# Chaining the shared products of a fast strided convolution and its gradient, and two passes of GELU instead of one for the second batch

## The chip, the cores and the metric

One core of one Trainium2 chip. The metric is the device time of one execution in microseconds (us), the median of the runs shown; lower is better. TensorE (PE) multiplies matrices into PSUM, VectorE (DVE) and ScalarE (ACT) do elementwise work, GpSimd (POOL) clears small ranges and issues some DMAs, and SyncE's queue (SP) issues nearly all DMAs.

## The reference

The forward part is a 1-D convolution with stride 2 and 31 taps over 256 channels, a normalisation of every channel over the sequence, and a tanh-approximated GELU. The kernel returns that output and the four gradients for a given `grad_out`.

```
B, T, D, K = 2, 16000, 256, 31            # L = 7985 outputs per batch
h = einsum('blc,cd->bld', x[:, 0:2*L:2, :], w[0])
for i in range(1, K):
    h = h + einsum('blc,cd->bld', x[:, i:i+2*L:2, :], w[i])
mu  = sum_l h / L
var = sum_l (h - mu)**2 / L
h   = (h - mu) / sqrt(var + 1e-5)
out_0 = gelu(h * gn_gamma + gn_beta)      # approximate=True
# out_1..out_4: gradients of x, w, gn_gamma, gn_beta for grad_out
```

Everything is bf16 in memory; the matmuls accumulate in fp32.

## The kernel before, in words

**Stages.** F is the convolution h (batch 0 is F0, batch 1 is F1), G the gradient of x (G0 and G1), W the gradient of w. Each batch is cut into four chunks, 0 to 3, of 2048 output positions. h and dy (the gradient at the normalised value) go through DRAM tensors `h_d` and `dy_d`.

**A fast convolution.** The tap number is split into bits, i = 8q + 4·r2 + 2·r1 + parity, and on r1, on r2 and on the lowest bit of q a two-by-two product is formed with three products instead of four, from sums and differences of inputs and of weights. The first split gives three *branches* B, A, C (`br`), worked in that order; the second gives three *leaves* B, A, C of each branch (`lf`). Inside a leaf the last split has a *shared product*, which uses a difference table of the weights (`WD`, in G and its counterpart `W2D…`) and counts for the even and the odd outputs alike, and two further products (`f_three_ac`, `g_three_ac`) with input combinations built by `third`. A leaf without that last split is done in full (`f_leaf`, `g_leaf`). One pass over a (batch, chunk, branch) is called a *unit* here; in G a chunk has two halves (`pr` = 0, 1), hence 48 units.

**PSUM.** A unit has two accumulators of two banks, `px` and `pt`; two pairs alternate. Leaf B of a branch is part of both results, so px is first filled with leaf B, then px goes on with leaf A and pt, seeded from px by `f_seed`, with leaf C.

**Units with all three leaves split (`outer`, set `FO`).** 14 of the 24 units of F: all of batch 0 except its very first, and chunk 3 of batch 1. Here `f_three_b` (L524) makes B's shared product and ScalarE spreads it over px with three copies (L540). `f_outer` (L556) makes A's and C's shared products side by side in pt, and ScalarE writes each to SBUF in both signs (`TS`, four copies of 512, L574). For branches A and C, DVE then adds the kept result of branch B (`RB`, fp32) to both (L641, 2048 elements, fp32), and two more DVE operations seed pt and px (L584, L588). `f_evac` moves a finished leaf: branch B into `RB` (L599), A and C into the bf16 tile `hs` with sums (L619) and, after the second leaf, sums of squares (L632).

**G.** Batch 1 has all leaves split (`GOC`, `g_outer`); batch 0 has only leaf B split, and the others go through `g_leaf`. The tables for the split leaves, `W2DC` and `W2DO`, are built by `w2_outer` (L1194, L1197) in the last chunk of batch 0. They lie in the memory (from `GREG` on) in which `gelu_batch` works for batch 1 and, above it, in that of a ring of tiles (`DNO`) from which `dl_turn` stores transposed leaves for W.

**GELU.** `gelu_unit` (L854) handles 1024 positions: it reads h, forms y = scale·h + bias and its square on ScalarE (L864, L866), a cubic on DVE (L869, one `scalar_tensor_tensor`), two sigmoids on ScalarE (L871, L873), then products on DVE (L875, L879): out_0's value y and dy. DVE's L892 and ScalarE's L890 make the sums for the parameter gradients. Batch 0's eight such passes run in F1, batch 1's eight in G0. For batch 1, y goes to DRAM (`y_d`), and `out0_late` (L912) reads it back with a DMA transpose in W and stores out_0. `e_comp` (L967) turns dy and h into the input of G: two scalings, an add on DVE (L985), and four copies by ScalarE into the tile `et` (L994).

**Order.** `Plan.add` collects 3252 operations with their dependences, and `emit` issues them in the order of `SEQUENCE`, a list of all their numbers. That list fixes the order in every queue; each engine and the SP queue then work strictly in that order.

Of the kernel before, what the change touches and what calls it, by code (L numbers as in the profile page):

```python
# [17 lines left out]
GELU_A = 0.044715  # L18
# [213 lines left out]
def conv_stem_kernel(  # L232
# [38 lines left out]
    gamma, beta = gbf[:, 0, :], gbf[:, 1, :]  # L271
    dgb_acc = cpool.tile([P, 2, 2], FP32, name="dgb_acc")
    eps_t = cpool.tile([P, 1], FP32, name="eps_t")
    stats = cpool.tile([P, NB, 8, 2], FP32, name="stats")
    small = cpool.tile([P, NB, 16, 2], FP32, name="small")
    hsum = [cpool.tile([P, 2, 17], FP32, name=f"hsum{b}") for b in range(NB)]
    hsq = [cpool.tile([P, 2, 8], FP32, name=f"hsq{b}") for b in range(NB)]
# [1363 lines left out]
```

## Time and profile before

| | |
|---|---|
| median of 3 runs | 1148.08 us (1147.48 to 1148.45) |
| profiled execution | 1147.09 us, of which its span (first to last instruction) 1145.0 us |
| TensorE clock granted, mean | 0.999 |
| PE busy | 1121.4 us, 98% of the span |
| DVE busy | 943.7 us, 82% |
| ACT busy | 561.7 us, 49% |
| POOL busy | 129.2 us, 11% |
| DMA | 243.56 MB, 213 GB/s on average |

The page of the profile has one row per group of instructions: line, engine, operation, output from input, and count, then busy time, mean ns of one, and idle time of the engine ahead of them with what ended it. Matmuls are pipelined, so the mean ns of one matmul is its latency and not its share of time; the share follows from how many stand in a stretch without a pause. The chain of waits lists, from the last instruction backwards, what released each step. A view by windows gives busy time, granted clock and DMA share in stretches of the span.

### The profile page before, as it was taken

Reading aid. Unit: us, or ns where it says so; the run is one execution under the profiler, and the core shown is the slowest. Engines: PE = TensorE matmul, PEld = TensorE weight load, DVE = VectorE, ACT = ScalarE, POOL = GpSimd, SP = SyncE. Lnnn points to the kernel's source line nnn. Section 1 sums busy time; section 2 is a strip of 40 time slices with the busy share of each in tenths; the row PEclk is TensorE's granted clock in tenths of the full one; section 3 lists DMA queues with packets and bytes.
Section 4 is the critical chain, followed back from the end, with each engine's and each line's share of the span. In section 5 each row is a group of like instructions: output and inputs, shape, how many; then the busy total and the mean of one; then the engine's idle time right before and its main releaser. Section 6 shows DMA issues by size and latency. Waiting matters only on the chain.

```text
span 1145.0 us, 18889 instructions
## 1 busy us (share of the span) xinstructions
PE 1121.4 (98%) x7645; PEld 753.0 (66%) x7700; DVE 943.7 (82%) x880; ACT 561.7 (49%) x873; POOL 129.2 (11%) x221
## 2 busy tenths in 40 slices
PE   5999999999999999999999999999999999999998
PEld 3888899877777874444444444444488766666785
DVE  7997877798999997999887654645599899789995
ACT  1235454777787488888663576754412212112200
POOL 0000000000000012133324325222200000000000
PEclk9999999999999999999999999999999999999999
DMA  9638867958897689999979877577899946989665
GB/s 231 114 80 167 165 161 180 190 123 203 175 207 181 221 333 248 274 268 268 254 185 238 214 204 202 154 191 193 221 302 234 288 149 209 311 260 348 195 218 150
DMA packets 345806, 243.56 MB, mean 213 GB/s; under 512 B 233377, under 2 KB 316967, under 8 KB 341543
## 3 DMA queue, kind: packets, MB, share of 16 engines
q1 hardware_dynamic: 338615, 223.47, 73.9%
q0 software_dynamic: 7104, 18.89, 5.9%
q8 instruction: 60, 0.98, 0.4%
q14 instruction: 27, 0.22, 0.1%
HBM read 106.24 MB, written 80.25 MB: 163 GB/s over the span
## 4 chain that ended last, share of the span: by engine, by line
PE 89%; DVE 7%; ACT 1%; issue 1%; DMA 1%; SPq 0%; DVEq 0%; ACTq 0%
PE ps L504 34%; PE ps L1099 33%; PE ps L1311 22%; DVE arena L1279 1%; DVE arena L1397 1%; DVE ps L1421 1%; DVE arena L1381 1%; DMA out_dram<-arena 1%; DVE arena L1045 1%; DMA arena<-in_x_dram 1%; DVE arena L446 0%; DVE arena L1482 0%; DVE arena L462 0%; ACT arena L994 0%; DVE arena L879 0%
## 5 line engine op out<-in xcount | busy, mean ns | idle before, releaser
L504 PE MATMUL ps<-arena 128*128 128x256 bf16 (+4 forms) x3460 | 406.0, 281 | 12.1 <-DVE arena L446 6.6
L1099 PE MATMUL ps<-arena 128*128 128x512 bf16 x1880 | 408.2, 377 | 3.0 <-DVE arena L1180 0.5
L504 PEld LDWEIGHTS <-arena 128*128 128x128 bf16 x3460 | 338.2, 98 | 79.8 <-DVE arena L446 7.0
L1099 PEld LDWEIGHTS <-arena 128*128 128x128 bf16 x1920 | 188.0, 98 | 222.5 <-issue 2.3
L1311 PE MATMUL ps<-arena 128*128 128x256 bf16 (+1 forms) x2305 | 307.8, 296 | 3.7 <-DVE arena L1477 2.6
L1311 PEld LDWEIGHTS <-arena 128*128 128x128 bf16 x2320 | 226.8, 98 | 84.8 <-issue 3.0
L599 ACT ACTIVATE arena<-ps 128x1024 f32<-128x1024 f32 (+1 forms) x111 | 112.6, 1023 | 234.4 <-PE ps L1311 82.8
L462 DVE TENSOR_TENSOR arena<-arena 128x2064 bf16<-128x2064 bf16 (+8 forms) x126 | 155.7, 1266 | 17.1 <-PE ps L504 16.0
L311 POOL DMA_DIRECT2D dld<-arena x144 | 104.3, 726 | 239.0 <-DMA arena<-arena 194.6
L879 DVE TENSOR_TENSOR arena<-arena 128x2048 bf16<-128x2048 bf16 (+1 forms) x80 | 95.3, 1197 | 8.6 <-ACT arena L871 4.5
L1279 DVE TENSOR_TENSOR arena<-arena 128x4096 bf16<-128x4096 bf16 x38 | 86.4, 2289 | 12.4 <-DMA arena<-in_x_dram 7.8
L1045 DVE TENSOR_TENSOR arena<-arena 128x1032 bf16<-128x1032 bf16 (+1 forms) x108 | 82.2, 791 | 9.7 <-PE ps L1099 9.3
L1162 DVE TENSOR_TENSOR ps<-ps,arena 128x1024 f32<-128x1024 f32 x24 | 29.5, 1231 | 59.0 <-PE ps L1099 36.3
L619 ACT ACTIVATE arena<-ps 128x512 bf16<-128x512 f32 (+1 forms) x64 | 37.1, 582 | 51.9 <-PE ps L504 48.4
L320 POOL MEMSET arena<- 128x128 bf16 (+11 forms) x40 | 8.9, 247 | 446.3 <-DVE arena L879 176.3
L1128 ACT COPY ps<-ps 128x512 f32<-128x512 f32 x72 | 41.5, 577 | 28.4 <-PE ps L1099 25.5
L1413 ACT COPY ps<-ps 128x256 f32<-128x256 f32 x54 | 19.3, 359 | 70.6 <-PE ps L1311 69.5
L574 ACT ACTIVATE arena<-ps 128x512 f32<-128x512 f32 x56 | 30.6, 601 | 44.2 <-PE ps L504 30.5
L869 DVE SCALAR_TENSOR_TENSOR arena<-arena 128x2048 bf16<-128x2048 bf16 (+1 forms) x16 | 35.8, 2240 | 16.7 <-ACT arena L864 10.7
L540 ACT ACTIVATE ps<-ps 128x256 f32<-128x256 f32 x75 | 27.8, 371 | 38.9 <-PE ps L504 38.0
L1180 DVE TENSOR_TENSOR arena<-ps,arena 128x1024 bf16<-128x1024 f32 x32 | 38.9, 1220 | 8.5 <-PE ps L1099 6.4
L1397 DVE TENSOR_TENSOR arena<-arena 128x2048 bf16<-128x2048 bf16 x36 | 43.4, 1222 | 0.1
(84 smaller groups left out, 772.6 us busy)
## 6 DMA issues: line engine op xcount, KB each, us to landing
arena<-in_x_dram SPq DMA_DIRECT2D x40, 1024.0 KB
dld<-arena POOLq DMA_DIRECT2D x144, 128.0 KB, 4.0
arena<-hd SPq DMA_DIRECT2D x32, 512.0 KB
out_dram<-arena SPq DMA_DIRECT2D x14, 1024.0 KB
arena<-dld SPq DMA_DIRECT2D x18, 640.0 KB
arena<-dld SPq DMA_DIRECT2D x18, 576.0 KB
vl<-arena SPq DMA_DIRECT2D x36, 256.0 KB
arena<-vl SPq DMA_DIRECT2D x9, 1024.0 KB
```

What stands on the lines that cost most here:

```text
L311: lambda: e.dma_start(out=out, in_=in_), dma=np_ * ns / 16e3 * 1.03, ns=ns, tp=SH[pk], slack=slack)
L462: lambda: nc.vector.tensor_tensor(out=o, in0=a, in1=b, op=ALU.add))
L504: yield nc.tensor.matmul(ps[:, dh, cs], lhsT=wt, rhs=mv, start=s0, stop=False, skip_group_check=True)
L599: lambda: nc.scalar.activation(out=out, in_=ps, func=ACT.Copy, scale=scale))
L879: add("DVE", dve(nf), [o], [a, b_], lambda: V.tensor_tensor(out=o, in0=a, in1=b_, op=op))
L1045: lambda: nc.vector.tensor_tensor(out=o, in0=a, in1=b, op=ALU.subtract))
L1099: yield nc.tensor.matmul(ps[:, e, 0:wide], lhsT=lt, rhs=mv, start=s0, stop=False, skip_group_check=True)
L1128: add("ACT", act(512), [o], [i], lambda: nc.scalar.copy(out=o, in_=i))
L1180: lambda: nc.vector.tensor_tensor(out=ho[:, :, k, :], in0=ps[:], in1=g, op=ALU.add))
L1279: add("DVE", dve(4096), [o], [a, b], lambda: nc.vector.tensor_tensor(out=o, in0=a, in1=b, op=ALU.add))
L1311: yield nc.tensor.matmul(ps[:, s, c0:c1], lhsT=lt, rhs=mv, start=s0, stop=False, skip_group_check=True)
L1397: add("DVE", dve(2048), [o], [u, v], lambda o=o, u=u, v=v: nc.vector.tensor_tensor(out=o, in0=u, in1=v, op=ALU.subtract))
```

## The change

1. *Convolution.* `f_outer` is gone. In an outer unit `f_shared` makes A's shared product in `pt`, ScalarE copies it into px's first bank, and `f_three_b` accumulates B's shared product on top of it. C's shared product is then accumulated on A's in `pt`, and ScalarE writes the sum out in both signs (two copies instead of four). `f_seed` shrinks to one operation: pt = TS − px, or, in units without outer leaves, a ScalarE copy for all branches. `RB` becomes bf16 and is added on DVE in `f_evac`, after branch A's and C's second leaf is in `hs`.
2. *Gradient.* `GOC` takes in chunk 3 of batch 0 (six units), and `w2_outer` builds its tables one chunk earlier.
3. *GELU.* For batch 0 the `scalar_tensor_tensor` becomes a `tensor_scalar` and a `tensor_tensor`. Batch 1 has a new `gelu_short`, which makes only dy, with the scales folded into extra per-channel constants, and both sums on ScalarE; the DRAM tensor `y_d` is gone. `out0_late` reads h again in W and applies ScalarE's own tanh-GELU.
4. *`e_comp`.* The add and the four copies become four adds on DVE that write `et` directly.
5. One step of the first chunk's PE transposes uses another PSUM pair, and `SEQUENCE` is a new list of all, now 3287, operations.

```diff
-    def f_three_b(ps, br, lf, op, co, we):
+    def f_shared(ps, br, lf, op, co, we, wd, fresh=True):
...
-                        jobs.append((0, slice(HM * dh, HM * dh + n), WD[br, lf][:, ch, q2, par, dh * P:(dh + 1) * P],
-                                     op[:, 1, o0:o0 + n], dh + q2 + par + ch == 0))
+                        jobs.append((0, slice(HM * dh, HM * dh + n), wd[br, lf][:, ch, q2, par, dh * P:(dh + 1) * P],
+                                     op[:, 1, o0:o0 + n], fresh and dh + q2 + par + ch == 0))
...
+    def f_three_b(ps, br, lf, op, co, we, fresh=True):
+        f_shared(ps, br, lf, op, co, we, WD, fresh)
...
+            v, g = hs.rearrange("p d e k f -> p (d e) k f")[:, :, br2:br2 + 3:2, 0:wd], RB.rearrange("p l a f -> p a l f")[:, :, :, 0:wd]
+            add("DVE", dve(8 * wd), [v], [v, RB], lambda: nc.vector.tensor_tensor(
+                out=v, in0=v, in1=g, op=ALU.add if br == A else ALU.subtract))
...
-    def f_seed(br, px, pt, outer, ts):
+    def f_seed(px, pt, outer, ts):
         vx, vt = flat2(px), flat2(pt)
...
+        if outer:
+            ve(vt, ts.rearrange("p d f -> p (d f)"), vx, ALU.subtract)
         else:
+            keep(vt, vx, -1.0)
...
+                    if outer:
+                        second(A)
+                        f_shared(pt, br, A, ops[A], co, we, wd)
+                        f_copy(px[:, 0], pt[:, 0])
                     third(B_, us[B_])
+                    if last and outer:
                         last(s0)
+                    f_three_b(px, br, B_, ops[B_], co, we, not outer)
                     if outer:
+                        second(C_)
+                        f_shared(pt, br, C_, ops[C_], co, we, wd, False)
+                        v = pt[:, 0].rearrange("p (d f) -> p d f", d=2)
+                        for e, sc in ((0, 1.0), (1, -1.0)):
+                            f_copy(ts[:, :, HM * e:HM * e + HM], v, sc)
                         third(s0, us[s0])
...
+        plus(z, 1.5)
+        tt(z, z, y, ALU.mult)
+        sig(s, 1.0 / 3.0)
+        tt(y, z, y, ALU.subtract)
+        sig(z, -1.0 / 3.0)
+        tt(y, y, z, ALU.mult)
+        plus(y, 1.0)
+        tt(y, y, s, ALU.mult)
+        tt(s, y, go, ALU.mult)
...
+        tt(y, s, h, ALU.mult)
...
     def out0_late(c, off):
...
+            load(t.rearrange("p d k f -> p d (k f)"), hv, 524288, 2048)
+            for dh in range(2):
+                v, sc, bi = t[:, dh], st(b, 2, dh), st(b, 3, dh)
+                add("ACT", act(1024, 0.18), [v], [v, sc, bi], lambda v=v, sc=sc, bi=bi: nc.scalar.activation(
+                    out=v, in_=v, func=ACT.Gelu_apprx_tanh, bias=bi, scale=sc))
+                turn(oo[:, :, dh * P:(dh + 1) * P], v.rearrange("p k f -> p (k f)"), 262144)
+            out0_store(b, c, e, oo)
...
-    GOC = {(1, c, pr) for c in range(NCK) for pr in range(2)}
+    GOC = {(1, c, pr) for c in range(NCK) for pr in range(2)} | {(0, 3, pr) for pr in range(2)}
...
-            w2_outer(A)
             e_load(1, 0)
...
-        if (b, c, pr, br) == (0, 3, 1, A) and GOC:
+        if (b, c, pr, br) == (0, 2, 1, A):
             w2_outer(C_)
+            w2_outer(A)
```

More of the change, by code (lines that the diff above doesn't have):

```diff
@@ L263, in conv_stem_kernel @@
     dy_d = [[dram.tile([P, 4096], BF16, name=f"dyd{b}_{c}") for c in range(NCK)] for b in range(NB)]
-    y_d = [dram.tile([D, 2048], BF16, name=f"yd{c}") for c in range(NCK)]
     dl_d = [[dram.tile([2, 1056, D], BF16, name=f"dld{b}_{i}") for i in range(9)] for b in range(NB)]
@@ L273, in conv_stem_kernel @@
     eps_t = cpool.tile([P, 1], FP32, name="eps_t")
-    stats = cpool.tile([P, NB, 8, 2], FP32, name="stats")
+    stats = cpool.tile([P, NB, 12, 2], FP32, name="stats")
     small = cpool.tile([P, NB, 16, 2], FP32, name="small")
@@ L815, in fwd_stats @@
         tiny([biy], [beta, tm], lambda: V.tensor_tensor(out=biy, in0=beta, in1=tm, op=ALU.subtract))
+        if b == 1:
+            for k, sc in ((7, 4.0 * GELU_C), (9, float(np.sqrt(1.5 * GELU_A)))):
+                for j, v in enumerate((scy, biy)):
+                    o = st(b, k + j)
+                    tiny([o], [v], lambda o=o, v=v, sc=sc: V.tensor_scalar(out=o, in0=v, scalar1=sc, scalar2=None, op0=ALU.mult))
     def gelu_batch(b, base, rings, ngt, noo, base0, pace):
@@ L823, in ring_of @@
             return [sb(base - (n - j) * size, *shape) for j in range(n)]
-        hs_, ys_, ss_, y2s, zs = (ring_of(k, 2, 4, HM) for k in rings)
+        tiles = [ring_of(k, 2, 4, HM) for k in rings]
         gts = ring_of(ngt, 4, 2, XM)
@@ L867, in gelu_unit @@
         nf = 8 * wd
-        add("DVE", dve(nf, 1), [z], [y2, y],
-            lambda: V.scalar_tensor_tensor(out=z, in0=y2, scalar=1.0 / GELU_A, in1=y, op0=ALU.add, op1=ALU.mult))
+        add("DVE", dve(nf, 4), [y2], [y2],
+            lambda: V.tensor_scalar(out=y2, in0=y2, scalar1=1.0 / GELU_A, scalar2=None, op0=ALU.add))
+        add("DVE", dve(nf), [z], [y2, y], lambda: V.tensor_tensor(out=z, in0=y2, in1=y, op=ALU.mult))
         add("ACT", act(nf), [s], [z],
@@ L894, in gelu_unit, with gelu_short, plus, tt @@
         yf = full[1].rearrange("p d k f -> p d (k f)")
-        if b == 0:
+        for dh in range(2):
+            turn(oo[:, :, dh * P:(dh + 1) * P], yf[:, dh], 262144)
+    def gelu_short(b, c, e, tiles, go, oo):
+        V, SC = nc.vector, nc.scalar
+        wd = HM if c < 3 else 232
+        full = tiles
+        h, y, s, z, go = (t[:, :, :, 0:wd] for t in (*tiles, go))
+        hv, dv = (d[b][c][:].rearrange("p (d e f) -> p d e f", d=2, e=2)[:, :, e] for d in (h_d, dy_d))
+        load(full[0].rearrange("p d k f -> p d (k f)"), hv, 524288, 2048, "ACT")
+        for dh in range(2):
+            for o, k, fn in ((y, 7, ACT.Identity), (z, 9, ACT.Square)):
+                sc, bi = st(b, k, dh), st(b, k + 1, dh)
+                add("ACT", act(4 * wd, 0.18), [o[:, dh]], [h[:, dh], sc, bi],
+                    lambda o=o, dh=dh, sc=sc, bi=bi, fn=fn: SC.activation(out=o[:, dh], in_=h[:, dh], func=fn, bias=bi, scale=sc))
+        nf = 8 * wd
+        def plus(o, k):
+            add("DVE", dve(nf, 4), [o], [o], lambda: V.tensor_scalar(out=o, in0=o, scalar1=k, scalar2=None, op0=ALU.add))
+        def tt(o, a, b_, op):
+            add("DVE", dve(nf), [o], [a, b_], lambda: V.tensor_tensor(out=o, in0=a, in1=b_, op=op))
+        def sig(o, sc):
+            add("ACT", act(nf), [o], [z], lambda: SC.activation(out=o, in_=z, func=ACT.Sigmoid, scale=sc))
+        plus(z, 1.5)
[7 more added lines that the diff above has]
+        tt(s, y, go, ALU.mult)
+        load(dv, full[2].rearrange("p d k f -> p d (k f)"), 524288, 2048, "POOL")
+        tt(y, s, h, ALU.mult)
+        u = 2 * c + e
+        for i, t, jk in ((0, s, h), (1, y, y)):
             for dh in range(2):
-                turn(oo[:, :, dh * P:(dh + 1) * P], yf[:, dh], 262144)
-        else:
-            load(y_d[c].rearrange("(d p) f -> p d f", p=P)[:, :, 1024 * e:1024 * e + 1024], yf, 524288, 2048, "POOL")
+                a0, v, j = esum[b][:, dh, i, u:u + 1], t[:, dh], jk[:, dh]
+                add("ACT", act(4 * wd, 0.19), [j, a0], [v],
+                    lambda j=j, v=v, a0=a0: SC.activation(out=j, in_=v, func=ACT.Copy, accum_out=a0))
     def out0_store(b, c, e, oo):
@@ L954, in dgb_store @@
             load(out.rearrange("(dh p) -> dh p", p=P), DGT[2 * i:2 * i + 2, :], 512, 256, "POOL", slack=500.0)
-    COPY = ("ACT", "ACT")
     def e_load(b, c):
```

139 lines of the change are left out of this document (48 added, 91 removed), and 205 rows, old and new, of the table SEQUENCE.

## The prediction

> **What bounds the kernel now.** I read the page first, then the chain of waits in order of time, then groups by line and shape, then the first 50 us engine by engine.
>
> ```profile
> span 1145.0 us, 18889 instructions
> ...
> PE 1121.4 (98%) x7645; PEld 753.0 (66%) x7700; DVE 943.7 (82%) x880; ACT 561.7 (49%) x873; POOL 129.2 (11%) x221
> ...
> L504 PE MATMUL ps<-arena 128*128 128x256 bf16 (+4 forms) x3460 | 406.0, 281 | 12.1 <-DVE arena L446 6.6
> L1099 PE MATMUL ps<-arena 128*128 128x512 bf16 x1880 | 408.2, 377 | 3.0 <-DVE arena L1180 0.5
> ```
> ```profile
> 21.46 391.13 PE ps L504 x3328
> ...
> 452.39 10.74 PE ps L1099 x49
> 463.19 10.31 PE ps L1099 x49
> ...
> 832.60 6.68 DMA out_dram<-arena
> ```
> ```profile
> 1140.32 0.42 DVE arena L1340
> ```
>
> PE is idle for 23.6 us of 1145.0. The first stretch of the convolution runs 391 us without a pause. So TensorE bounds every stage. Idle time lies before 21.5 us (about 12), at the change to W (a DMA of 6.68 us is on the chain) and in the 4.7 us after the last matmul. An edit helps by the matmuls it removes and by shortening those ends; what it takes from DVE or ACT is only cover.
>
> **Gradient of x: the one place where matmuls go.** A unit with only leaf B split has 4 + 8 + 16 + 16 = 44 matmuls of 512 columns; with all leaves split 4 + 4 + 4 + 8 + 8 + 8 = 36. In branch A some are half as wide, so there it is 42 against 35. Six units change: 2 × (8 + 8 + 7) = 46 fewer. All of G now has 24 × 44 + 24 × 36 = 1920 matmuls, worth 1896 full widths; 408.2 us / 1896 = 0.2153 us each (the two chain rows give 0.210 and 0.219). **46 × 0.2153 = 9.9 us off PE**, on PE's own path, nothing hiding it. The convolution keeps its number: 32 matmuls of `f_outer` become two times 16.
>
> **Convolution.**
>
> ```profile
> L641 DVE TENSOR_TENSOR arena<-arena 128x2048 f32<-128x2048 f32 x10 | 22.9, 2291 | 8.1 <-ACT arena L574 7.6 <-ACT arena L599 0.5
> L584 DVE TENSOR_TENSOR ps<-ps,arena 128x1024 f32<-128x1024 f32 x28 | 34.2, 1226 | 4.3 <-PE ps L1311 4.3
> L1176 DVE TENSOR_TENSOR arena<-arena 128x2048 bf16<-128x2048 bf16 x16 | 19.5, 1220 | 11.6 <-ACT arena L599 11.5
> L574 ACT ACTIVATE arena<-ps 128x512 f32<-128x512 f32 x56 | 30.6, 601 | 44.2 <-PE ps L504 30.5 <-DVE arena L584 6.1 <-DVE arena L462 5.0
> L540 ACT ACTIVATE ps<-ps 128x256 f32<-128x256 f32 x75 | 27.8, 371 | 38.9 <-PE ps L504 38.0
> L599 ACT ACTIVATE ps<-ps 128x1024 f32<-128x1024 f32 x29 | 29.2, 1007 | 23.1 <-PE ps L1099 16.0 <-DVE arena L1180 3.8 <-PE ps L1311 3.0
> ```
>
> DVE loses ten adds of 2.291 (22.9) and 40 seeds of 1.226 (49.0); it gets 14 seeds (17.2) and 16 bf16 adds of 1.220 (19.5): −35 us. ACT loses 14 copies of 0.601 (8.4) and gets 6 of 1.007 (6.0): −2. PE gains nothing, since it has no pause here. What is added is a wait: `f_three_b` must follow a 0.60 us copy that follows `f_shared`, 14 times. Queued behind it on PE is the rest of that unit. Uncovered it would cost 14 × 0.6 = 8.4 us; counted in the new order list, one to six other groups of matmuls (8 × 0.109 = 0.87 us or more) stand between the two each time. The nearest row is L540: 25 triples of such copies (3 × 0.371 = 1.1 us) stand between the same kinds of matmul, and PE does not wait. I take 0.3, bounds 0 and 8.4.
>
> **Start.**
>
> ```profile
> 12.22 5.09 PE L504 MATMUL ps<-arena 128*128 128x512 bf16 x24 [2.47 <-DVE arena L446]
> 21.46 23.74 PE L504 MATMUL ps<-arena 128*128 128x256 bf16 x192 [4.15 <-DVE arena L446]
> ```
> ```profile
> 15.52 15.09 DVE L446 TENSOR_TENSOR arena<-arena 128x2048 bf16<-128x2048 bf16 x13
> ```
> ```profile
> 2.85 13.94 SPq L311 DMA_DIRECT2D arena<-in_w_dram  x16
> ```
> ```profile
> 22.00:24.00 2.00, 2.00 (x12) 1.38 (x11) 2.00 (x3) 0.00 (x0) 0.00 (x0) 0.50 1.54 164
> 24.00:26.00 2.00, 2.00 (x11) 1.09 (x10) 1.97 (x3) 1.10 (x3) 0.00 (x0) 0.65 0.54 100
> ```
> ```profile
> 450.00:500.00 50.00, 49.74 (x231) 23.00 (x235) 49.55 (x57) 41.07 (x48) 11.79 (x19) 1.00 1.02 283
> ```
>
> At 21.46 PE waits for the fifth of the 13 weight subtractions, 15.09 / 13 = 1.16 us each. In the new list two of the four ahead of it stand behind it: −2.3. But one weight load now stands ahead of the first loads of x on SP: 13.94 / 16 = 0.87 later. Then PE meets the two displaced subtractions and others: 1.75 us of matmuls against 2 × 1.16, twice, and once more later, 1.3 in all. And after the 4.15 us pause the clock was 0.50 for 2 us and 0.65 for 2: 1.7 us of work lost. The new pause is 4.15 − 2.3 = 1.8 us. Stretches of G with pauses of some 0.25 us in 50 stay at 1.00 (last row), so I take it that the loss goes: −2.3 + 0.9 + 1.3 − 1.7 = −1.8, rounded to **−1.6** since the load of the last weights may bind instead. Bounds: −3.2 (no new gaps) and +0.9 (only the delay is left).
>
> The Trainium skill, "TensorE: Matmul & The Clock Gate", Part 1 on the HAM clock gate, says that the clock halves after an idle window of about 3.4 us; the 4.15 us pause with 0.50 behind it agrees. By it a pause of 1.8 us keeps the clock, and the same rule speaks against the change if a new stall grows beyond 3.4 us.
>
> **Gelu, `e_comp`, and the gradient's tables.**
>
> ```profile
> L879 DVE TENSOR_TENSOR arena<-arena 128x2048 bf16<-128x2048 bf16 x60 | 73.0, 1222 | 7.9 <-ACT arena L871 4.5 <-ACT arena L873 1.9
> L869 DVE SCALAR_TENSOR_TENSOR arena<-arena 128x2048 bf16<-128x2048 bf16 x12 | 27.5, 2289 | 11.5 <-ACT arena L864 6.0 <-ACT arena L866 5.3
> L875 DVE TENSOR_SCALAR arena<-arena 128x2048 bf16<-128x2048 bf16 x12 | 8.3, 692 | 0.2
> L892 DVE CUSTOM_DVE_ANT_0 arena<-arena 128x1024 bf16<-128x1024 bf16 x24 | 28.9, 1220 | 0.2
> L864 ACT ACTIVATE arena<-arena,stats 128x1024 bf16<-128x1024 bf16 x24 | 29.0, 1231 | 4.3 <-DVE stats L815 2.1 <-DVE arena L879 2.0 <-issue 0.2
> L871 ACT ACTIVATE arena<-arena 128x2048 bf16<-128x2048 bf16 x12 | 22.9, 1909 | 7.7 <-DVE arena L869 7.5
> L890 ACT ACTIVATE arena<-arena 128x1024 bf16<-128x1024 bf16 x24 | 25.1, 1046 | 5.2 <-DVE arena L879 5.0
> L890 ACT ACTIVATION_READ_ACCUMULATOR arena<-arena 128x1 f32 x32 | 6.0, 189 | 0.0
> L994 ACT COPY arena<-arena 128x768 bf16<-128x768 bf16 x32 | 25.9, 830 | 9.1 <-DVE arena L985 7.7 <-POOL arena L320 1.4
> L1197 DVE SCALAR_TENSOR_TENSOR arena<-arena 128x2048 bf16<-128x2048 bf16 x3 | 6.9, 2284 | 0.0
> L450 DVE TENSOR_TENSOR arena<-arena 128x1024 bf16<-128x1024 bf16 x20 | 13.4, 684 | 0.0
> ```
> ```profile
> 411.99 1.02 PE L1099 MATMUL ps<-arena 128*128 128x512 bf16 x3
> 412.85 6.11 PE L504 MATMUL ps<-arena 128*128 128x231 bf16 x60
> ```
> ```profile
> 429.43 2.37 ACT L866 ACTIVATE arena<-arena,stats 128x1024 bf16<-128x1024 bf16 x2
> ```
> ```profile
> 591.77 1.11 DVE L892 CUSTOM_DVE_ANT_1 arena<-arena 128x928 bf16<-128x928 bf16 x1
> ```
>
> One pass of batch 1 costs DVE 2.289 + 0.692 + 5 × 1.222 + 2 × 1.220 = 11.5 now and 2 × 0.692 + 6 × 1.222 = 8.7 after; ACT gets two sums more, 2 × (1.046 + 0.189) = 2.5. Each `e_comp` call moves two copies of 0.830 and two shorter ones to DVE, about +0.45 there (estimated between the 1024 row, 0.684, and the 2048 row, 1.222). DVE at 49.55 of 50 falls by some 6; ACT at 41.07 about holds. PE has no wait here now, so no gain.
>
> The new dependence is in time. The tables of the six units lie where batch 1's gelu works. G starts at 411.99, with 6.1 us of convolution still in between, and 18 units are 6 × (44 + 42 + 44) × 0.2153 = 167.9: chunk 3 starts at 586.0. Gelu's last sum ended at 592.9, eight passes of (592.9 − 429.4) / 8 = 20.4 us. By the new list the second unit's first shared product stands 11.3 us into the chunk, at 597.3; its table needs the last h tile free (two more sums on ACT, 2.5) and 1.22 to build: 596.6 (the tables of leaf A, 2.284 each, come after gelu's product with grad_out and are needed later). At the old pace it just fits, with 0.7 us to spare. A pass has a chain of 2 × 1.231 + 1.222 + 2 × 1.909 + 1.222 + 0.692 + 3 × 1.222 + 2.5 = 15.6 us, so 20.4 holds 4.8 of queueing, which a lighter DVE shortens; gelu's start comes some 2 us later (a bf16 add ahead of each last sum of squares, four tiny scalings). I take **0.5** lost here; bounds 0 and the rivals below.
>
> **W.**
>
> ```profile
> 820.00:850.00 30.00, 27.38 (x212) 20.61 (x212) 27.38 (x25) 8.48 (x13) 0.00 (x0) 1.00 0.86 268
> 850.00:900.00 50.00, 49.61 (x454) 44.04 (x452) 50.00 (x33) 12.46 (x21) 0.00 (x0) 1.00 0.99 271
> ```
> ```profile
> 1104.66 4.24 SPq L316 DMA_TRANSPOSE arena<-yd  x1
> ```
>
> ACT gets 16 gelus of 1.23 us, where 8.48 of 30 us are busy. SP issues 8 loads, 16 transposes and twice the stores in place of 4 transposes of 4.24 us; no row has so small a transpose, and the bytes stay equal, so 1.06 each or more. Behind a transpose that waits for its gelu on SP stand the loads of W's tiles, for which DVE and then PE wait. The DMAs move 4 MB more here, and 4 MB less in G. I take 0.2; bounds 0 and 6.7 (the DMA wait of 832.60 once more).
>
> **Sum.** 1147.09 − 9.9 − 1.6 + 0.3 + 0.5 + 0.2 = 1136.6 for the profiled execution; it lies 1.0 under the median of 1148.08, so the forecast is **1137.6 us**.
>
> **Rivals.**
> 1. *The gelu of batch 1 gets slower and chunk 3 waits for its tables: slower than before.* For: ACT takes 2.5 us more per pass in a chain that already passes 592.9, and only 0.7 us is spare. Against: DVE is the fuller engine and loses 2.8 a pass. It turns at a lateness of 0.7 + 10.5 + 2.3 = 13.5 us, a pace of 22.1; a stall that long also costs the 1.7 us of clock. At 22.9 per pass (ACT's 2.5 fully on the chain, 8 × 2.5 = 20 late): 1137.6 + 19.3 − 0.5 + 1.7 = 1158. Chance 0.04.
> 2. *The pace stays and the start is later by 3 to 6 us:* that is PE's wait, 1140 to 1143. For: the little spare. Against: the load on DVE. Chance 0.18.
> 3. *W's SP queue blocks behind a transpose:* up to 6.5 more, 1139 to 1144. Against: PE is busy 49.61 of 50 us right after, where the DMA share is 0.99. Chance 0.08.
> 4. *The start gains 3.2 and nothing new waits:* 1135. Chance 0.12.
>
> The forecast with its small terms, 1136 to 1140, has 0.58.
>
> **How the numbers follow.** A measurement can tell about 0.2% (2.3 us) from no change, so faster means below 1145.8. Cases 2, 3, 4 and the forecast all lie below: 0.93, with 0.03 taken off for two of the costs meeting, which is the chance of the same; slower 0.04. The range 1134.5 to 1142.6 leaves out rival 1 and the upper parts of 2 and 3, some 0.14.
>
> **What would show it.** Weight loads of L1099's successor should be 1872 instead of 1920, with about 398 us of matmul time and 0.215 each. F should show no pause of PE after the start, DVE's share there lower. PE's second pause should be below 3 us with the clock at 1.00 after it. Between 575 and 600 PE should wait less than 1 us; a wait there on DVE's table building is rival 1 or 2. In W, ACT has 16 gelus and one table load, and PE no new DMA wait. I am wrong if G gets shorter by clearly less than 9 us, or if a stage other than the start changes by more than 2.

## The result and the profile after

The changed kernel takes **1141.69 us** (median of 4 runs, 1141.02 to 1143.5), the kernel before 1148.26 us beside it: a ratio of 0.9942, 95% interval 0.9923 to 0.996. That is 6.6 us less; the forecast was 10.5 less, 1137.6. The profiled execution took 1141.57 us with a span of 1139.8. Intervals here and below leave out the one slow run, of `drain_first` (1179.62 us at a granted clock of 0.947).

The page of the changed kernel (its line numbers are 20 higher in G and W; busy time and mean ns, then idle time ahead and what ended it):

```profile
span 1139.8 us, 18854 instructions
...
PE 1112.9 (98%) x7599; PEld 747.3 (66%) x7652; DVE 897.4 (79%) x905; ACT 572.9 (50%) x868; POOL 130.1 (11%) x233
...
L1119 PE MATMUL ps<-arena 128*128 128x512 bf16 (+1 forms) x1833 | 398.7, 376 | 4.9 <-DVE small L959 1.3
...
L1119 PEld LDWEIGHTS <-arena 128*128 128x128 bf16 x1872 | 183.2, 98 | 219.6 <-issue 3.2
```

Weight loads say what was issued: 1872 in G, 48 fewer, which are the forecast's 46 full widths, since some in branch A are half as wide. PE is 8.5 us less busy, DVE 46 less, and the idle time ahead of G's matmuls rises from 3.0 to 4.9. Next PE's timeline: of the changed kernel the start, then from the first product of G (411.37) to the first of W (821.27); last, of the kernel before, the two places of G with a pause. Columns are start, duration, and in brackets the pause ahead with what ended it.

```profile
5.82 4.09 PE L504 MATMUL ps<-arena 128*128 128x128 bf16 x48 [5.82 <-DMA arena<-in_x_dram]
13.36 6.29 PE L504 MATMUL ps<-arena 128*128 128x512 bf16 x24 [3.45 <-DVE arena L462]
20.46 1.93 PE L504 MATMUL ps<-arena 128*128 128x256 bf16 x16 [0.81 <-DVE arena L446]
```
```profile
411.37 1.03 PE L1119 MATMUL ps<-arena 128*128 128x512 bf16 x3
412.92 6.11 PE L504 MATMUL ps<-arena 128*128 128x231 bf16 x60 [0.53 <-DVE ps L568]
...
580.16 11.38 PE L1119 MATMUL ps<-arena 128*128 128x512 bf16 x51 [0.52 <-DVE arena L1200]
592.83 1.04 PE L1119 MATMUL ps<-arena 128*128 128x512 bf16 x4 [1.29 <-DVE small L959]
594.57 5.34 PE L1119 MATMUL ps<-arena 128*128 128x512 bf16 x24 [0.70 <-ACT ps L1148]
600.21 221.22 PE L1119 MATMUL ps<-arena 128*128 128x512 bf16 x1011 [0.30 <-ACT arena L572]
821.27 3.66 PE L1331 MATMUL ps<-arena 128*128 128x256 bf16 x32
```
```profile
442.23 5.34 PE L1099 MATMUL ps<-arena 128*128 128x512 bf16 x24 [0.38 <-ACT ps L599]
448.08 380.86 PE L1099 MATMUL ps<-arena 128*128 128x512 bf16 x1748 [0.51 <-DVE arena L1180]
```

Cut at these two points and at the last matmul (1140.27 before, 1134.19 after), the span falls into four pieces that can be set against the forecast (us):

| piece | before | after | forecast | measured |
|---|---|---|---|---|
| start and convolution | 411.99 | 411.37 | −1.3 | −0.6 |
| G | 416.79 | 409.90 | −9.4 | −6.9 |
| W | 311.49 | 312.92 | +0.2 | +1.4 |
| after the last matmul | 4.73 | 5.61 | 0 | +0.9 |
| span | 1145.0 | 1139.8 | −10.5 | −5.2 |

All four pieces came out 0.7 to 2.5 us above the forecast. In G the six units of chunk 3 begin at 580.16, and that is where four of its five new pauses are: 0.52, 1.29, 0.70 and 0.30. (The fifth, 0.53 at 412.92, stands ahead of the last products of the convolution.) DVE's timeline there, of the changed kernel:

```profile
590.36 1.22 DVE L450 TENSOR_TENSOR arena<-arena 128x2048 bf16<-128x2048 bf16 x1
...
591.56 1.22 DVE L1200 TENSOR_TENSOR arena<-ps,arena 128x1024 bf16<-128x1024 f32 x1
592.69 0.15 DVE L959 TENSOR_TENSOR small<-small 128x2 f32<-128x2 f32 x1
```

L1200 empties the PSUM tile that the product at 592.83 writes; the tiny L959, on which the pause is put, comes right behind it. Ahead of it stand a table step (L450) and small steps of gelu's end, and DVE has no pause from 576 to 608 us.

### The profile page after: what moved, and what is told of

Read it like the earlier page. It is cut to its first block, busy times and chain, and to the rows that moved or that the text cites. A ratio compares the mean times of both kernels' runs of the same rounds, so it can differ in the third digit from the quotient of the medians.

```text
span 1139.8 us, 18854 instructions
## 1 busy us (share of the span) xinstructions
PE 1112.9 (98%) x7599; PEld 747.3 (66%) x7652; DVE 897.4 (79%) x905; ACT 572.9 (50%) x868; POOL 130.1 (11%) x233
## 5 line engine op out<-in xcount | busy, mean ns | idle before, releaser
L1119 PE MATMUL ps<-arena 128*128 128x512 bf16 (+1 forms) x1833 | 398.7, 376 | 4.9 <-DVE small L959 1.3
L572 ACT ACTIVATE arena<-ps 128x1024 bf16<-128x1024 f32 (+1 forms) x119 | 120.6, 1023 | 238.1 <-PE ps L1331 67.6
L462 DVE TENSOR_TENSOR arena<-arena 128x2080 bf16<-128x2080 bf16 (+8 forms) x126 | 156.5, 1265 | 32.3 <-PE ps L504 31.1
L1065 DVE TENSOR_TENSOR arena<-arena 128x1032 bf16<-128x1032 bf16 (+1 forms) x111 | 86.7, 801 | 4.3 <-PE ps L1119 3.8
L1182 DVE TENSOR_TENSOR ps<-ps,arena 128x1024 f32<-128x1024 f32 x30 | 36.9, 1230 | 58.7 <-PE ps L1119 48.7
L538 ACT ACTIVATE ps<-ps 128x256 f32<-128x256 f32 (+1 forms) x89 | 35.8, 404 | 69.6 <-PE ps L504 68.6
L902 DVE TENSOR_TENSOR arena<-arena 128x2048 bf16<-128x2048 bf16 (+1 forms) x48 | 57.4, 1197 | 5.9 <-ACT arena L895 3.0
L320 POOL MEMSET arena<- 128x78 bf16 (+11 forms) x52 | 11.5, 244 | 402.5 <-DVE arena L462 256.7
L864 DVE TENSOR_TENSOR arena<-arena 128x2048 bf16<-128x2048 bf16 (+1 forms) x40 | 47.7, 1198 | 10.9 <-ACT arena L856 6.5
L1200 DVE TENSOR_TENSOR arena<-ps,arena 128x1024 bf16<-128x1024 f32 x24 | 29.2, 1220 | 19.1 <-PE ps L1119 14.0
L1502 DVE TENSOR_TENSOR arena<-arena 128x4608 bf16<-128x4608 bf16 x16 | 40.7, 2548 | 0.0
L572 ACT ACTIVATE ps<-ps 128x1024 f32<-128x1024 f32 x29 | 29.3, 1009 | 21.3 <-PE ps L1119 10.4
```

The source lines that it names most:

```text
L462: lambda: nc.vector.tensor_tensor(out=o, in0=a, in1=b, op=ALU.add))
L572: lambda: nc.scalar.activation(out=out, in_=ps, func=ACT.Copy, scale=scale))
L864: add("DVE", dve(nf), [o], [a, b_], lambda: V.tensor_tensor(out=o, in0=a, in1=b_, op=op))
L902: add("DVE", dve(nf), [o], [a, b_], lambda: V.tensor_tensor(out=o, in0=a, in1=b_, op=op))
L1065: lambda: nc.vector.tensor_tensor(out=o, in0=a, in1=b, op=ALU.subtract))
L1119: yield nc.tensor.matmul(ps[:, e, 0:wide], lhsT=lt, rhs=mv, start=s0, stop=False, skip_group_check=True)
```

## The experiments

The theory after this result: the matmuls saved what was computed; in G some 2.5 us came back because DVE, full at the start of chunk 3, frees PSUM late; in W and at the end 2.3 us came back through the late out_0; at the start the late rows of x took back the gain. The main rival for G: gelu of batch 1 ends too late for the tables (the prediction's rivals 1 and 2), or the matmuls were worth less than computed.

In the edits, numbers are operations in the order list. 1839, 1851 and 1858 empty PSUM (L1200); 1860, 1900 and 1922 are seeds (L1182); 1825 and 1826 are tables (L450), 1828 and 1829 the slower ones (L1217); 1431 to 1445 are gelu's last small steps; 1863 to 1868 scale and add the first half of the next batch's input, behind which its second half is loaded; 1422 is a gelu step; the other DVE numbers are G's sums (L1065), and 1855 and 1856 on PE are products of G.

### The six units undone

```
-    GOC = {(1, c, pr) for c in range(NCK) for pr in range(2)} | {(0, 3, pr) for pr in range(2)}
+    GOC = {(1, c, pr) for c in range(NCK) for pr in range(2)}
```

> The six units of chunk 3 of batch 0 in the gradient of x go back to 44, 42 and 44 matmuls; everything else stays as in the changed kernel, the tables too, which are built at the same places. Theory (the saving is real, and about 2.5 us of it are lost in the hand-off of the first all-split units): the matmul group of the gradient grows by 9.5 to 9.9 us, the pauses of PE between 580 and 601 us (2.8 us in the changed kernel) shrink to 0.5, so G takes 417 us instead of 409.9 and the time is 1148.5. Rival 1 (the pauses come from DVE's load alone, the tables and the small steps at gelu's end, whatever the units do): the pauses stay and the time is 1151. Rival 2 (the removed matmuls were worth less than 0.215 us each): the matmul group grows by 7 us only, and the pauses stay as they were.

Measured 1159.33 us, ratio 1.0101 (1.0086 to 1.0116): more than any case. Its G matmuls, and PE's timeline:

```profile
L1118 PE MATMUL ps<-arena 128*128 128x512 bf16 (+1 forms) x1880 | 410.3, 377 | 9.5 <-ACT arena L571 2.9 <-ACT ps L1147 2.8 <-ACT ps L571 1.4
```
```profile
665.98 1.02 PE L1118 MATMUL ps<-arena 128*128 128x512 bf16 x4 [2.92 <-ACT arena L571]
667.71 32.45 PE L1118 MATMUL ps<-arena 128*128 128x512 bf16 x141 [0.71 <-ACT ps L1147]
```

Behind 666 us the granted clock was 0.73, 0.50 and 0.92 in three windows of 2 us, 1.7 us lost. The matmul group is 11.6 us above the changed kernel's 398.7; less 1.7 that is **9.9, the forecast's term**, so rival 2 is out (that it fits to the tenth is luck: the 1.7 is read from three rows). The pauses are another matter: G is 426.1 us, 16.2 more, of which 9.9 are matmuls, 1.7 clock and 4.6 more pauses, where the theory had fewer. They stand behind ScalarE's copies: 4.3 us in three pauses behind L571 and 2.8 in four behind L1147. The likely reason, which no run here tests, is that the list, made for split units, leaves no other work for PE at these places. Undoing one part under a list made for the other is no clean control; the matmul group is, the time is not, and on the cause of the changed kernel's own pauses this run says nothing.

### DVE's order at the start of chunk 3: three tries and a doubled step

First try, everything that PE waits for ahead of all the rest:

```
 DVE
-1422 1839
+1839 1422
-1851 1901 1431 1902 1432 1825 1433 1858 1434 1438 1435 1436 1904 1439 1860 1440 1442 1441 1443 1444 1445
-1903 1864 1863 1865 1826 1866 1905 1867 1828 1868 1829 1900 1906 1922
+1851 1825 1858 1860 1901 1902 1904 1826 1903 1828 1905 1900 1829 1906 1922
+1431 1432 1433 1434 1438 1435 1436 1439 1440 1442 1441 1443 1444 1445 1864 1863 1865 1866 1867 1868
 PE
-1855 1856
+1856 1855
```

> Only the order of DVE's and two of PE's instructions around the start of chunk 3 of batch 0 (about 578 to 606 us): DVE empties the PSUM tiles and writes the seeds first, the six table steps come as they are needed, and the fourteen small steps of gelu's end and the sums of the next batch go behind. Theory (PE waited because what frees its PSUM tiles stood behind tables and small steps on DVE): the pauses 0.52, 1.29 and 0.70 shrink to 0.7 in all, PE is busy 49 of 50 us in 550 to 600 instead of 47.19, G is 1.8 us shorter, time 1139.9. Rival 1 (gelu of batch 1 itself ends too late, so that the table of the second unit sets the time whatever the order): the pauses stay within 0.4 us, 1141.7. Rival 2 (the load only moves): the pauses go, but the delayed sums of the next batch make PE wait near 630 us, 1141 to 1143.

Measured 1148.78 us, ratio 1.0003 (0.9993 to 1.0013): the whole gain was gone. PE's and DVE's timelines:

```profile
593.46 5.34 PE L1119 MATMUL ps<-arena 128*128 128x512 bf16 x24 [0.70 <-ACT ps L1148]
...
606.86 12.90 PE L1119 MATMUL ps<-arena 128*128 128x512 bf16 x59 [2.41 <-DVE arena L1217]
623.01 77.23 PE L1119 MATMUL ps<-arena 128*128 128x512 bf16 x339 [3.26 <-DVE ps L1182]
```
```profile
603.38 1.23 DVE L1182 TENSOR_TENSOR ps<-ps,arena 128x1024 f32<-128x1024 f32 x1 [3.54 <-ACT arena L1148]
604.52 2.28 DVE L1217 SCALAR_TENSOR_TENSOR arena<-arena 128x2048 bf16<-128x2048 bf16 x1
...
618.27 0.75 DVE L1000 TENSOR_SCALAR arena<-arena,stats 128x2048 bf16<-128x2048 bf16 x1 [2.87 <-DMA arena<-dyd]
...
621.73 1.22 DVE L1182 TENSOR_TENSOR ps<-ps,arena 128x1024 f32<-128x1024 f32 x1
```

The pause of 1.29 is gone, as the theory has it. But two orders were wrong. Seed 1900 waits for a copy of ScalarE and stood ahead of table 1829, so DVE idled 3.54 us with the table behind it, and PE 2.41. And the last of the next batch's sums came 11 us late, so did the loads behind them, and a seed (621.73) stood behind a scaling (L1000) that waited 2.87 us for such a load; PE waited 3.26. G is 416.8 us, 6.9 more, with what the clock lost behind the second pause (0.50 from 624 to 628). Rival 2 had named the second wait (near 630), but with 1141 to 1143 in all. DVE takes its queue strictly in order: what waits in front holds all that stands behind. (The Trainium skill, "TensorE: Matmul & The Clock Gate", in its opening table, calls DVE's queue strictly first in, first out; this run agrees.)

Second try, less:

```
 DVE, against the changed kernel
 1839 before 1422; 1825 1858 1860 right behind 1851; 1866 1867 1868 behind 1900
 PE
-1855 1856
+1856 1855
```

> Less is moved than in drain_first: on DVE one table step, one emptying and the seed behind it go ahead of the small steps of gelu's end, one emptying goes ahead of a gelu step, and the last three sums of the next batch go behind the last table and the seed after it; the loads of the next batch's second half start some 3 us later, not 11. Theory (DVE is full from 576 to 606 us, and what frees PSUM must come first, what only has to be done by 612 us after it): the pauses of PE between 578 and 606 us fall from 2.8 to some 1.5 us, none appears near 607 and near 623, G is 1.3 us shorter, 1140.4. Rival 1 (DVE is simply too full there: what is gained at 593 is lost at the last table, about 605): 1141.7, with a pause of about 1 us before a product that needs the last table. Rival 2 (any delay of the next batch's sums hits the loads behind them): a pause above 2 us near 620, 1143 or more.

Measured 1142.24 us, ratio 0.9946 (0.9924 to 0.9967), G 410.0 us. PE's timeline:

```profile
593.01 5.34 PE L1119 MATMUL ps<-arena 128*128 128x512 bf16 x24 [0.70 <-ACT ps L1148]
600.03 50.28 PE L1119 MATMUL ps<-arena 128*128 128x512 bf16 x228 [1.69 <-DVE arena L450]
```

Rival 1 was right in kind: the pause moved from 592.8 to 600.0, where the next table (1826) is waited for, and not the last, as it had said. The doubled step says the same from the other side; table 1825 is built twice:

```
+                def go(o=o, x0=x0, x1=x1, n=2 if br == A else 1):
+                    for _ in range(n):
+                        yield nc.vector.tensor_tensor(out=o, in0=x0, in1=x1, op=ALU.add)
```

> One table step of DVE, the one of 1.22 us near 590 us, is done twice, with the same result; nothing else changes. Theory (DVE is full from 576 to 606 us, and what PE waits for near 592.8 stands behind this step): the pause there grows by 1.1 us, from 0.9 to 1.3 up to 2.0 to 2.4, the other pauses stay, time 1142.8; if the clock is cut behind the longer pause, 1.7 us more. Rival (DVE has slack there, and PE waits for gelu's last sums on ACT or for a copy): the pauses stay as they were, 1141.7.

Measured 1143.66 us, ratio 0.9961 (0.9945 to 0.9976). PE's timeline:

```profile
593.80 1.89 PE L1119 MATMUL ps<-arena 128*128 128x512 bf16 x4 [2.36 <-DVE small L959]
596.39 7.29 PE L1119 MATMUL ps<-arena 128*128 128x512 bf16 x24 [0.70 <-ACT ps L1148]
```

The step adds 1.1 us of DVE, the pause grows by 1.1 (from 1.29), and the matmuls behind it run at a lower clock (7.29 us where they took 5.34; 0.50 from 594 to 600 us). So DVE's queue, not gelu, sets this pause. Gelu was early: in the changed kernel its last sum on ScalarE ended at 588.5, where the prediction feared 595. Third try, with `store_early` (below) in it:

```
 DVE, against drain_first
-1905 1900 1829 1906 1922 1431 to 1445 1864 1863 1865 1866 1867 1868
+1905 1431 to 1445 1864 1863 1829 1900 1865 1866 1867 1868 1906 1922
```

> store_early, and a third order of DVE at the start of chunk 3: the emptying of PSUM, the seed and the tables first, in the order in which the products use them, then gelu's small steps, then the sums of the next batch, split around the last table and a seed, so that the loads behind them start some 1 to 2 us later than in the changed kernel, not 11 as in drain_first. Theory: pauses of PE in 576 to 606 us of about 1.5 us instead of 2.8, G 1 us shorter than 409.6, and the end as in store_early: 1138.5. Rival (DVE's sum of work there sets the time, as in drain_less): the pauses move but their sum stays 2.3 to 2.8, 1139.5.

Measured 1140.19 us, ratio 0.9933 (0.9915 to 0.995). G's pauses:

```profile
580.95 11.38 PE L1119 MATMUL ps<-arena 128*128 128x512 bf16 x52 [0.29 <-ACT ps L572]
593.04 5.34 PE L1119 MATMUL ps<-arena 128*128 128x512 bf16 x24 [0.70 <-ACT ps L1148]
598.68 5.35 PE L1119 MATMUL ps<-arena 128*128 128x512 bf16 x24 [0.30 <-ACT arena L572]
604.73 45.55 PE L1119 MATMUL ps<-arena 128*128 128x512 bf16 x212 [0.70 <-DVE arena L1217]
```

2.0 us instead of 2.8, and G 409.06 instead of 409.90: in the trace some 0.8 us, but the median isn't below `store_early` alone. So 1.8 of the changed kernel's 2.8 us (0.52 and 1.29) are DVE's queue, and a better order of DVE gives back less than half of that. Of the 2.0 that are left, 0.70 ends on DVE, at a table (L1217), and 1.29 at copies of ScalarE. The pause of 0.70 at 593.04 is among these and stands in every run with these units: the list puts product 1888 straight behind product 1886 on PE, with nothing between but ScalarE's copy (0.57 us) of the one for the other. No run changed that, and what DVE's sum of work costs beyond its order stays open.

### The end of the span

```
 SP
-3272 3213 3263 3273 3264 3191 3228 3229
+3213 3228 3229 3272 3263 3273 3264 3191
```

3213, 3228 and 3229 are the last stores of out_0, the others stores of out_2.

> Only SP's order at the end: the last three stores of out_0 go ahead of five stores of out_2 that wait for DVE. Theory (the end of the span is later by 0.9 us because the last stores of out_2 queue behind stores of out_0): from the last matmul to the end 4.8 us instead of 5.6, time lower by 0.8, 1140.9. Rival (the wires are full at the end with the same bytes, or the stores of out_0 are simply late): no change, 1141.7, with the DMA share above 0.7 up to the end.

Measured **1139.52 us**, ratio 0.9926 (0.9911 to 0.9941), all 4 runs (1139.39 to 1140.28) below all of the changed kernel's. The windows of the end (busy times, then clock, DMA share and GB/s), first of the changed kernel, then with the stores moved:

```profile
1128.00:1132.00 4.00, 4.00 (x35) 3.21 (x34) 2.46 (x2) 0.00 (x0) 0.00 (x0) 1.00 0.14 39
...
1136.00:1138.00 2.00, 0.00 (x0) 0.00 (x0) 0.00 (x0) 0.00 (x0) 0.00 (x0) 1.00 0.76 220
```
```profile
1128.00:1132.00 4.00, 4.00 (x36) 3.32 (x34) 2.46 (x2) 0.00 (x0) 0.00 (x0) 1.00 0.55 141
...
1136.00:1138.00 2.00, 0.00 (x0) 0.00 (x0) 0.00 (x0) 0.00 (x0) 0.00 (x0) 1.00 0.08 23
```

Finished stores of out_0 stood on SP behind stores of out_2 that waited for DVE: the DMA share was 0.14 while there was something to send, and 0.76 when all else was over. Now 3.9 us follow the last matmul, less than the 4.7 of the kernel before; so the theory's 0.8 was too small, and it had the two the wrong way round: out_0 was held up by out_2. The ratios of the two kernels overlap (0.9911 to 0.9941, 0.9923 to 0.996), but the traces agree: 5.6 to 6.1 us follow the last matmul in the nine profiled runs with the old order and the late output, 3.8 or 3.9 in the three with the new one. No complete kernel here has a lower median.

The other half, out_0 of batch 1 not written:

```
-            if n in LATE:
+            if n in ():
```

> Leaves out the output out_0 of batch 1: its 16 gelus on ScalarE, their loads, transposes and stores in W. Everything before W stays. Theory (W and the end are longer because of this added work: 312.9 instead of 311.5 us of W, 5.6 instead of 4.7 us after the last matmul): W 311.5 to 311.8 us, 3.9 us after the last matmul as in store_early, 1138.7. Rival 1 (W's pauses come from DVE's order and data of the earlier stage, not from out_0): W stays 312.5 or more, only the end gets shorter, 1140.0. Rival 2 (SP's queue blocked W's loads, as feared in the prediction): W falls below 310 us, 1136.

Measured 1138.84 us, ratio 0.9919 (0.99 to 0.9938). W is 311.7 us (822.97 to 1134.65), where the twelve profiled runs with that work have 312.3 to 313.7, mean 312.9, and the end is 3.9 us. The theory holds: the late output costs W about 1.2 us (one profiled run against twelve), and its stores the end 1.7. Rival 2, a blocked load, does not show.

### The start

```
 SP: 26 and 15 are weights, 12, 13 and 11 loads of x
-26 12 13 15 11
+12 13 26 15 11
```

> Only SP's order at the start: the weight load that stands ahead of the first two loads of x goes behind them. Theory (the start is a chain x rows, transposes, DVE; the rows came 1.2 us later): first matmul at 4.6 to 5.2 us instead of 5.82, PE resumes after its second pause at 19.3 to 19.8 instead of 20.46, time lower by 0.6 to 1.2, about 1140.7. The pause ahead of the first convolution matmuls stays 3.4 or a little less, so the clock of 0.50 may or may not show. Rival (the weights bind: the subtractions wait for a load that now lands later): first matmul earlier, but PE resumes at 20.4 as before and the time stays at 1141.7.

Measured 1142.4 us, ratio 0.9957 (0.9942 to 0.9972). PE's timeline:

```profile
4.65 1.89 PE L504 MATMUL ps<-arena 128*128 128x128 bf16 x16 [4.65 <-DMA arena<-in_x_dram]
...
9.26 0.91 PE L504 MATMUL ps<-arena 16*128 16x16 bf16 x18 [0.73 <-DMA arena<-in_x_dram]
13.52 5.67 PE L504 MATMUL ps<-arena 128*128 128x512 bf16 x24 [3.35 <-DVE arena L462]
20.62 1.93 PE L504 MATMUL ps<-arena 128*128 128x256 bf16 x16 [1.43 <-DVE arena L446]
```

The first rows came 1.2 us earlier, but the last ones, the third load, not, and PE resumed at 20.62. All three ahead:

```
-26 12 13 15 11
+12 13 11 26 15
```

> Only SP's order at the start: all three loads of x first, then the two weight loads that had stood among them. Theory (in rows_first the third load of x, the last 16 rows, became the late one, and DVE works without a pause from its data on, so the start is as long as x is late): last transposes end near 8.9 us instead of 9.9 to 10.2, PE resumes after the second long pause at 19.5 to 19.9 instead of 20.5 to 21.5, the first product of the gradient starts near 410.6 instead of 411.4 to 412.4, time 1140.7. Rival (the weights now bind): DVE shows a wait for a weight load before 16 us, PE resumes at 20.5 or later, 1141.7.

Measured 1142.18 us, ratio 0.9944 (0.9926 to 0.9962): PE began at 4.58, waited 1.26 us for rows in between, and resumed at 21.03. So this delay isn't put right by SP's order. Then DVE's:

```
 DVE: 62 a weight subtraction, 66 half of a sum of x
-62 66
+66 62
```

> Only two of DVE's instructions change places at the start: the second half of the first sums of x goes ahead of one weight subtraction (0.6 us) that stood before it. Theory (the start is bound by DVE's total work up to the second long pause, and the clock of 0.50 after the first pause is covered by the wait for DVE): the pause before the first convolution matmuls falls from 3.35 or 3.45 us to about 2.8, the clock stays at 1.00 there, those 24 matmuls take 5.1 to 5.6 us instead of 6.3, the second pause grows by as much, and the time does not change: 1141.7. Rival (the clock loss at the start costs 1.2 us of the time): 1140.5.

Measured 1142.33 us, ratio 0.9945 (0.9928 to 0.9963). PE's timeline:

```profile
13.80 5.28 PE L504 MATMUL ps<-arena 128*128 128x512 bf16 x24 [2.85 <-DVE arena L462]
21.50 1.93 PE L504 MATMUL ps<-arena 128*128 128x256 bf16 x16 [2.42 <-DVE arena L446]
```

As the theory has it: the first pause is 0.6 shorter, the second longer, and PE resumes no earlier. In all nine profiled runs with the start of the changed kernel it resumes 7.09 or 7.10 us after its first convolution matmuls, whether these took 5.20 us or 6.50. The last try moved one sum of 1.23 us (85) behind the subtractions, put 66 ahead of 62 as above, and a cast (45) ahead of the first sum (67); two operations of DVE further on (74 and 109) moved too:

```
-67 45 61 62 66 68 84 65 85 64 83 69 63 70 71 73
+45 67 61 66 62 68 84 65 64 83 69 63 70 71 85 73
```

> both_orders, and at the start one sum of x of 1.23 us that is needed late goes behind the five weight subtractions for which PE waits, and the other sums as in sums_first. Theory (the start is as long as the DVE work ahead of those subtractions, since PE resumed 7.1 us after its first convolution matmuls in all runs with the same order of DVE): PE resumes 0.9 to 1.2 us earlier against its first convolution matmuls' old place, the first product of the gradient starts at 410.5 to 411.2 us, time lower by 0.9 than both_orders, 1137.6. Rival (the weights' loads bind, or PE only waits longer at the next subtraction): the first product at 411.4 to 412.4 as before, no gain over both_orders.

Measured 1140.43 us, ratio 0.9942 (0.9923 to 0.9962): no gain over `both_orders`. DVE's timeline shows the rival, the next thing in line:

```profile
18.08 7.27 DVE L446 TENSOR_TENSOR arena<-arena 128x2048 bf16<-128x2048 bf16 x6 [0.84 <-DMA arena<-in_w_dram]
```

With a sum less ahead of it, the subtraction waits for its weights.

### Is DVE only cover in the convolution?

```
+                for _ in range(3 if extra else 0):
+                    yield nc.vector.tensor_tensor(out=DUM, in0=DUM, in1=DUM, op=ALU.add)
```

> Behind the seeds of 12 of the 14 chained units of the convolution (all but the two of the first chunk) DVE does three additions more, of 896 float32 columns each, in a tile that nobody reads: 36 of about 1.07 us, 38 us in all, about what the chained products had taken off DVE there. Theory (the convolution's DVE work is only cover, TensorE has no pause there): no pause of PE above 0.6 us in 50 to 411 us, the first product of the gradient starts where it did (411.4 to 412.4 us), time 1141.7 as without them, within 0.5. Rival (the relief of DVE is part of the gain, by shorter hand-offs of seeds and sums): the first product of the gradient comes 2 us later or more, 1143.7 or more.

Measured 1169.71 us, ratio 1.0188 (1.0169 to 1.0207): the theory fell, by 28 us. PE's and DVE's timelines, then the window from 50 to 100 us of this run and of the kernel before:

```profile
89.79 6.30 PE L504 MATMUL ps<-arena 128*128 128x256 bf16 x56 [1.79 <-DVE arena L462]
```
```profile
84.11 1.23 DVE L624 TENSOR_TENSOR ps<-arena,ps 128x1024 f32<-128x1024 f32 x1 [1.56 <-ACT arena L538]
85.25 3.34 DVE L626 TENSOR_TENSOR arena<-arena 128x896 f32<-128x896 f32 x3
88.51 1.23 DVE L462 TENSOR_TENSOR arena<-arena 128x2064 bf16<-128x2064 bf16 x1
```
```profile
50.00:100.00 50.00, 46.23 (x419) 40.70 (x418) 43.63 (x40) 15.92 (x38) 0.00 (x0) 1.00 0.73 166
```
```profile
50.00:100.00 50.00, 50.00 (x458) 44.54 (x456) 43.93 (x38) 18.31 (x43) 0.00 (x0) 1.00 0.58 120
```

DVE is as busy in both (43.63 and 43.93 of 50 us), and PE loses 3.8 us here and has no pause in the kernel before. From 50 to 400 us DVE is even less busy here, 285.42 us against 305.56, and PE 336.25 of 350 against all of it. So the load alone isn't the cause. The three additions come in one piece behind a seed (84.11), and the sum (88.51) that PE needs next stands behind them. So the 35 us that the change took off DVE were cover where the list had placed them; as a free reserve, put anywhere, they don't exist. The start of chunk 3 keeps its pauses here (1.29 and 0.70, at 620.5 and 622.3, 27.7 us later): gelu, tables and products all come that much later, so this run doesn't part the two causes.

## Why the prediction was right in sign and too low

Two of the prediction's own signs speak against it in G, which got 6.9 us shorter, where clearly less than 9 was to count as wrong, and where PE waited 2.5 us between 575 and 600, not less than 1. The time lies inside the range, 1134.5 to 1142.6, but above the 1136 to 1140 that the forecast with its small terms was given, in the part left open for rivals 2 and 3. Neither happened, so that it lies inside is in part luck.

**The matmuls, −9.9: right.** The group of G fell by 9.5, and by 9.9 against the six units undone.

**The start and the convolution, −1.3 in all; −0.6 in the profiled execution.** Over the eight profiled runs that share this start (without `conv_load`) the first product of G comes at 411.4 to 412.4, mean 411.8, against 411.99: only −0.2. The step for the subtractions held (from the first convolution matmuls to the resumption 9.24 us before, 7.10 after: −2.1 for −2.3). The step "one weight load ahead, 0.87 later" failed: over the eight runs the rows of x came at 5.82 to 6.66, mean 6.1, against 4.59, and the first convolution matmuls 1.55 later (mean 13.77 against 12.22), but the rows are the smaller part of that. DVE's timeline, first of the kernel before, then of the changed one:

```profile
10.25 1.31 DVE L462 TENSOR_TENSOR arena<-arena 128x1040 bf16<-128x1040 bf16 x2
11.48 0.69 DVE L446 TENSOR_TENSOR arena<-arena 128x1024 bf16<-128x1024 bf16 x1
```
```profile
10.19 0.70 DVE L462 TENSOR_TENSOR arena<-arena 128x1040 bf16<-128x1040 bf16 x1 [0.58 <-ACT arena L406]
10.81 0.68 DVE L408 CAST arena<-ps 128x512 bf16<-128x512 f32 x1
11.41 1.28 DVE L446 TENSOR_TENSOR arena<-arena 128x1024 bf16<-128x1024 bf16 x2
```

DVE's first sum (L462) starts at 10.19 to 11.25 in the eight runs, mean 10.6: 0.35 later than before. From it to the first convolution matmuls it is 3.17 us in all eight and was 1.97, since a cast (L408) and a subtraction (L446) that stood ahead of this sum now stand behind it. These 1.2 us had no term in the forecast. `sums_first`, with the subtraction moved, has 2.57, and `all_orders`, with the cast moved too, 1.96; `rows_first` and `rows_all`, with early rows and that order of DVE, gain nothing.

From the resumption to the first product of G it is 390.91 us against 390.53 with the clock's 1.7 in it, so +2.1 without: new pauses of 0.34, 0.60, 0.23 and 0.30, and 0.6 that no pause shows, where the forecast had 1.3 and the 0.3 for the chained hand-off. The 1.7 of the clock did go: the second pause is 0.81 and the clock behind it 1.00. What the prediction did not see is that the first pause grows from 2.47 to 3.45 us, and that the clock may be 0.50 behind it in its turn (14 to 18 us in the changed kernel); the wait for DVE covers it.

**Gelu and the tables, +0.5: the step that failed most.** Named pauses of G rose from 0.89 to 3.34 us, +2.45; 2.81 of the 3.34 stand at the start of chunk 3. The prediction asked when the tables' memory comes free, and that was no problem: gelu ended at 588.5, not 595, though the second unit's first product was due at 591.5 (580.16 + 11.38), not at 597.3. It took DVE's load as an average that falls by 6 us in 50. From 576 to 608 us DVE was busy 31.75 of 32 us, where it had been 28.08 in the kernel before, and the queue there held tables, gelu's end, the next batch's sums, PSUM's emptying and the seeds. What waited there was the emptying of PSUM, which has no term in the forecast; the 0.70 behind a copy of ScalarE has none either. Its rivals 1 and 2 named the place but the wrong cause; rival 2's time, 1140 to 1143, came true without its mechanism.

**W, +0.2, and the end, 0: +1.4 and +0.9.** The prediction priced loads blocked behind transposes on SP. PE has no wait for a DMA in W, the 16 gelus need one table load, and rival 3 didn't happen. What it left out is that the late out_0 also ends late: its last stores are among the last things on SP, and the sum had no term for the time after the last matmul. The runs put 1.2 us on W and 1.7 on the end, and the order of stores gives back the latter.

**The share of each.** The forecast is 5.3 us too low for the profiled execution's span: 0.7 start and convolution, 2.5 G (2.0 pauses, the rest matmul time), 1.2 W, 0.9 the end.

## What to carry to other kernels

Where one engine is full for some 30 us, read its queue there instruction by instruction: ask of each instruction who waits for it, and of each that stands in front what it waits for itself; shares over 50 us hide both. Work that is moved to the end of a kernel has two prices, the engine's time and its place in the store queue; a store that is ready must not stand behind one that isn't. And a run that undoes a part tells by the group of instructions it changes, not by its total, when the order of everything else was made for that part.

## What the runs showed of the hardware

The granted clock after short pauses. The same pauses in two runs, 1.26 or 1.29 us, 1.04 us of matmuls, 0.70 us: in the changed kernel the 24 matmuls behind them took 5.34 us, in `rows_first` 7.03, with this window:

```profile
596.00:598.00 2.00, 2.00 (x6) 0.76 (x5) 1.97 (x4) 0.57 (x1) 2.00 (x4) 0.51 1.03 387
```

Of seven runs with about these pauses (0.94 to 1.29, then 0.70) two lost 1.7 us so (the other was `no_late_out0`). By the Trainium skill, "TensorE: Matmul & The Clock Gate", Part 1, activity is watched in a window of about 3.4 us that runs freely. That the same pauses had both outcomes fits this; no run here shows the window itself, and 1.96 us of pauses in 3.0 were enough, none of them near 3.4. At the start pauses of 2.6 to 3.5 us gave rows of 0.50 in some runs and 1.00 in others, and the matmuls' times don't follow these rows: 5.28 us for 24 matmuls with a row of 0.50 in `sums_first`, 5.67 with 1.00 in `rows_first`. What decides there stays open.
